# Query and key transposes from rearranged squares, relative decays, and a different start, in a fused retention and feed-forward kernel

## The chip, the core and the metric

The kernel runs on one core of one Trainium2 chip. The metric is the time of one execution on the device in microseconds (us), as the median of several runs. A profile of one execution shows the core's engines: PE is the matrix engine (PEld are its weight loads), DVE the vector engine, ACT the scalar engine, POOL the general engine, and SP the one that issues nearly all DMAs, on one queue (q1). A name with q behind it, such as SPq, is an engine's sequencer at work on instructions that are not counted as busy time, such as DMA issues.

## The reference

```python
batch, n_heads, seq, head_dim = (8, 8, 576, 64)          # q, k, v
scores = (1.0 / np.sqrt(D_)) * np.matmul(q, k.transpose(0, 1, 3, 2))
gamma = 1.0 - 2.0 ** (-5.0 - np.arange(H, dtype=np.float32))
rel = pos[:, None] - pos[None, :]
Dmat = np.where(rel >= 0, gamma[:, None, None] ** rel[None, :, :], 0.0)
attn = np.matmul(scores * Dmat[None], v)                  # (B, H, S, D)

x = attn.transpose(0, 2, 1, 3).reshape(4608, 512)
h = x @ w_in                                              # w_in 512 x 2048, float64
sp = np.maximum(h, 0.0) + np.log1p(np.exp(-np.abs(h)))
out = (h * erf(sp)) @ w_out                               # w_out 2048 x 512, float64
```

A retention layer (causal attention with one decay factor per head and no softmax) is followed by a feed-forward block. The inputs q, k, v are float32; the two weight matrices arrive as 64-bit floats and the kernel makes 32-bit floats of them itself ("rounding" below).

## The kernel before, in words

**Pieces and stages.** The retention is worked through in 40 pieces: 8 batches of 576 tokens, each cut into pieces of 128, 128, 128, 128 and 64 tokens. A piece has three stages. `transposes(i)` brings q and k into the layout with the head dimension on the partitions. `scores(i)` multiplies them and masks the product with the triangle `tri`. `outputs(i)` adds two terms in PSUM: masked scores times values (L323), and the running state times q (L334). It also multiplies keys with values (`kv`, L346) to bring the state up to date, and writes the result, scaled, into the token tile `x`. The stages are laid one over the other: transposes of piece i+1 come ahead of outputs of piece i, and scores of piece i+1 behind them. `attend(n)` issues stages up to number n, and `done[0]` counts them.

**Decays.** A power of gamma is split over two factors. Values are multiplied on POOL by a power that falls with the token's position in the whole batch (`weigh_values`, L276, table `gk`, which has one set for each of the five pieces). Outputs are multiplied by `gs` (start of the piece) and `gq` (position in it), in four instructions for a piece (L376). The state is a plain sum: for the first piece of a batch ACT copies `kv` into it (L358), later DVE adds `kv` to the old one (L360, L364).

**Transposes.** k is always transposed on PE, four matmuls with an identity for a piece (L296, tile `pt_k`), and ACT copies the result out of PSUM (L297). q goes the same way in batches 0 and 1. From batch 2 on, `load_squares` (L120, called at the first piece of the batch before) fetches the q of a whole batch by four DMAs in runs of 128 bytes (L125), laid out in squares of 32 by 32, so that one DVE instruction (L299), which transposes each 32 by 32 square, leaves the piece's q in the wanted layout.

**Loads.** `load(i)` issues the DMAs of a piece on SP (L115). Pieces 0 to 2 are asked for ahead of everything; at `transposes(i)` piece i+3 is asked for. The tiles of raw k and v have four buffers, raw q has two, so q is asked for one piece later than k and v.

**Weights.** `load_weights` fetches one part of a weight matrix (0.5 MB, L200) into one of three raw buffers. The generator `rounding` turns it into float32 in five steps a part: two ACT instructions (L217, L218), three steps of DVE (L222, L226, L230), then a last one with DVE (L235), two POOL instructions (L236, L237) and the load of a further part. After the last part of a group of four come four DVE additions (`sums_in` or `sums_out`), one a step. Four parts make the `wa` of a group (for `w_in`), four the `wb` (for `w_out`). `round_weights(n)` issues n such steps into the instruction streams at that point.

**Feed-forward.** The 4608 tokens are 9 chunks of 512, and the inner width is 4 groups; `order` takes all chunks for group 0, then for group 1 and so on. Each pair is a `First` (7 products of a Strassen-like scheme on `wa`, L432, and the activation with Softplus and Erf) and a `Second` (7 products on `wb`, L511). The retention runs among the feed-forward of group 0, a chunk ahead of it: `run` issues one or two stages ahead of each product. Results of a group are added up through `od` in DRAM.

**The start.** Up to the end of the first 512 tokens only retention stages are issued, one at a time, with two rounding steps after each from the second stage on (L585 to L587). Then come the products of `firsts[0]`, with two stages before each and one rounding step, then 4, 2 and 4 more steps around `firsts[1].first()`, and 9 at n == 1 (L620).

All engines take their instructions in the order in which the program issues them; nothing reorders them later. PSUM holds four tiles for the retention (`ps_at`), two for `a` and one each for `e` and `g`.

Of the kernel before, what the change touches and what calls it, by code (L numbers as in the profile page):

```python
# [11 lines left out]
FP32 = mybir.dt.float32  # L12
# [3 lines left out]
ALU = mybir.AluOpType  # L16
PSUM = bass.MemoryType.PSUM

P = 128
B, H, S, D = 8, 8, 576, 64  # L20
D_MODEL, D_FF = 512, 2048
NP = H // 2
NS = -(-S // P)
CONST_COLS = NS * H + NP * P + NS * NP + P

# [6 lines left out]
def decays():  # L32


    gamma = 1.0 - 2.0 ** (-5.0 - np.arange(H, dtype=np.float64))
    pairs = gamma.reshape(2, NP)
    t = np.arange(P)
    starts = np.arange(NS) * P
    gk = pairs.T.reshape(1, 1, H) ** -(starts[None, :, None] + t[:, None, None])
    row = pairs.repeat(D, axis=0)  # L40
    gq = row[:, :, None] ** t[None, None, :] / math.sqrt(D)
    gs = row[:, None, :] ** starts[None, :, None]
    tri = t[None, :] >= t[:, None]
    return np.concatenate([x.reshape(P, -1) for x in (gk, gq, gs, tri)], axis=1).astype(np.float32)
# [3 lines left out]
def kernel(  # L48
# [28 lines left out]
    wraw = ctx.enter_context(tc.tile_pool(name="wraw", bufs=3))  # L77
# [21 lines left out]
    loaded = {i: {} for i in range(len(pieces))}  # L99
# [3 lines left out]
    SQ = 32  # L103

    def load(i, names="kv"):
        if i >= len(pieces):
            return
        b, s0, n = pieces[i]
        for name, src in (("q", q), ("k", k), ("v", v)):
            if name in names and not (name == "q" and b >= SQUARES):  # L110
                bufs = 2 if name == "q" else 4
                t = raw.tile([P, H, D], FP32, tag=name, name=f"raw_{name}", bufs=bufs)
                for e in range(2):
                    heads = src[b, e * NP : (e + 1) * NP, s0 : s0 + n, :]
                    nc.sync.dma_start(out=t[:n, e::2, :], in_=heads.rearrange("h p d -> p h d"))  # L115
                loaded[i][name] = t

    squares = {}

    def load_squares(b):  # L120
        if SQUARES <= b < B:
            t = squares[b] = raw.tile([P, NP, S // SQ, SQ], FP32, tag="q4", name="raw_q4", bufs=2)
            for part in range(P // SQ):
                e, d0 = part // 2, part % 2 * SQ
                nc.sync.dma_start(  # L125
                    out=t[part * SQ : (part + 1) * SQ].rearrange("r p a d -> r (p a) d"),
                    in_=q[b, e * NP : (e + 1) * NP, :, d0 : d0 + SQ].rearrange("p (a r) d -> r (p a) d", r=SQ),
                )

    load(0, "qkv")  # L130
# [3 lines left out]
    for m in (NS * H, NP * P, NS * NP, P):  # L134
        ends.append(ends[-1] + m)
    gk, gq, gs, tri = (cst[:, a:b] for a, b in zip(ends, ends[1:]))
    gk = gk.rearrange("p (s h) -> p s h", s=NS)
    gq = gq.rearrange("p (a i) -> p a i", a=NP)
    load(1, "qkv")
# [103 lines left out]
    for _ in range(3):  # L243
        load_weights()
# [18 lines left out]
    x = {}  # L263
# [7 lines left out]
    def weigh_values(i):  # L271

        if i < len(pieces):
            _, s0, n = pieces[i]
            t = loaded[i]["v"]
            nc.gpsimd.tensor_tensor(  # L276
                out=t[:n],
                in0=t[:n],
                in1=gk[:n, s0 // P, :].unsqueeze(2).to_broadcast([n, H, D]),
                op=ALU.mult,  # L280
            )

    def transposes(i):
        b, s0, n = pieces[i]
        t = live[i] = loaded.pop(i)
        load(i + 3)
        load(i + 2, "q")
        if s0 == 0:
            load_squares(b + 1)
        weigh_values(i + 1)  # L290
        for name in "qk":
            tT = t[name + "T"] = att.tile([P, NP, P], FP32, tag=name + "T", name=name + "T")
            if name in t:
                pt = ps_at.tile([P, NP, P], FP32, tag="at", name=f"pt_{name}")
                for p in range(NP):
                    nc.tensor.transpose(pt[:, p, :n], flat(t[name][:n, 2 * p : 2 * p + 2, :]), ident[:n, :n])  # L296
                nc.scalar.copy(out=tT[:, :, :n], in_=pt[:, :, :n])  # L297
            else:
                nc.vector.transpose(  # L299
                    out=tT[:, :, :n].rearrange("p a (s i) -> p a s i", i=SQ),  # L300
                    in_=squares[b][:, :, s0 // SQ : (s0 + n) // SQ, :],
                )
# [14 lines left out]
    def outputs(i):  # L317
# [24 lines left out]
        if s0 + n < S:  # L342
            kv = ps_at.tile([P, NP, D], FP32, tag="at", name="kv")
            for p in range(NP):
                for e in range(2):
                    nc.tensor.matmul(  # L346
                        kv[e * D : (e + 1) * D, p, :],
                        lhsT=t["k"][:n, 2 * p + e, :],
                        rhs=t["v"][:n, 2 * p + e, :],
                        start=(p == 0),  # L350
                        stop=(p == NP - 1),
                        skip_group_check=True,
                    )
            old = kept.get("state")
            if pieces[i + 1][2] > D:
                new = att.tile([P, NP, D], FP32, tag="state", name="state")
                if s0 == 0:
                    nc.scalar.copy(out=new, in_=kv)  # L358
                else:
                    tt(new, kv, old, ALU.add)  # L360
            else:
                new = states[b % 2]
                for r in heads:
                    tt(new[r, :, r], kv[r], old[r], ALU.add)  # L364
            kept["state"] = new
        t0 = b * S + s0
        while t0 < b * S + s0 + n:
# [6 lines left out]
            for p in range(NP):  # L374
                j = s0 // P * NP + p
                nc.vector.scalar_tensor_tensor(  # L376
                    out=x[0, c][:, p, at],
                    in0=o[:, p, a : a + m],
                    scalar=gs[:, j : j + 1],
                    in1=gq[:, p, a : a + m],  # L380
                    op0=ALU.mult,
                    op1=ALU.mult,
                )
# [198 lines left out]

    weigh_values(0)
    while done[0] < stages_for(TCH):
        attend(done[0] + 1)  # L585
        if done[0] >= 2:
            round_weights(2)  # L587
# [5 lines left out]
    def run(steps, rounds=(), stages=1):  # L593

        for step, _ in enumerate(steps):
            attend(min(done[0] + stages, most[0]))
            if step in rounds:
                round_weights()

    run(firsts[0].first(), (0, 1), 2)  # L600
    run(firsts[0].middle(), (0, 1, 2), 2)
    run(firsts[0].last(), (0, 1), 2)
# [4 lines left out]
    round_weights(4)  # L607
    run(firsts[1].first(), (0, 1))
    firsts[0].multiply()
    round_weights(4)  # L610
    for b, nxt in zip(blocks[1:], blocks[2:] + [None]):
        n = order.index((b.g, b.c))
        if isinstance(b, First):
# [4 lines left out]
            run(b.middle(), (0, 1))  # L618
            firsts[n - 1].sums()
            if n == 1:  # L620
                round_weights(9)
            run(seconds[n - 1].first(), (0, 1))
            run(b.last())
            most[0] = stages_for(min((n + 3) * TCH, n_tok)) - (n + 3 < n_ch)
        elif n + 2 < n_s:
# [8 lines left out]
            run(nxt.first(), (0,))  # L634
            f.multiply()
            run(b.last(), (1,))
# [41 lines left out]
```

## Time and profile before

| quantity | value |
|---|---|
| median of 9 runs | 1090.33 us (1088.39 to 1091.72) |
| time of the profiled execution | 1088.99 us |
| its span | 1087.2 us |
| busy: PE, PEld, DVE, ACT, POOL | 1049.9, 901.1, 625.8, 397.0, 123.5 us |
| moved by DMA | 178.6 MB, 164 GB/s over the span |
| PE busy between 0 and 27 us | 11.71 us |
| PE busy between 27 and 54 us | 19.88 us |
| PE busy between 82 and 109 us | 21.98 us |
| PE busy between 136 and 1000 us | all of it |

The profile lists, for each group of instructions, its line, engine and operation, the tile it writes and those it reads, its shape and count, the busy time, the mean of one, and the idle time of the engine ahead of it with what ended that. In the timeline each row has the start, the time it took, engine, line, operation, tiles, count, and in brackets the idle time before it with the releaser. A row of windows has the stretch, its length, busy time and number of instructions of PE, PEld, DVE, ACT and POOL, the granted clock of PE as a share of full speed, the mean busy share of the 16 DMA engines (over 1 where packets of an engine overlap) and GB/s. With a tile named, the engines' columns count that tile's instructions alone.

### The profile page before, as it was taken

To read this page: it belongs to the slowest core of one execution; us is meant where nothing else is said; L and a number is where in the kernel's file an instruction comes from. 1 tells how busy PE (TensorE), PEld (TensorE's weight loads), DVE (VectorE), ACT (ScalarE), POOL (GpSimd) and SP (SyncE) were. 2 spreads that over 40 slices of the span, in tenths; PEclk is the share of its full clock that TensorE was granted. 3 is DMA by queue.
4 is the path that set the end of the run, shared out by engine and by line. 5 is a ranking of instruction groups with operands and counts; after the bars stand their busy time and mean duration, and the time that the engine had idled before them with its cause. 6 is when DMAs were issued, how large, how long until landed. Compare 5 with 4: busy or idle time off the path is not lost.

```text
span 1087.2 us, 15783 instructions
## 1 busy us (share of the span) xinstructions
PE 1049.9 (97%) x6472; PEld 901.1 (83%) x6472; DVE 625.8 (58%) x1074; ACT 397.0 (37%) x501; POOL 123.5 (11%) x110
## 2 busy tenths in 40 slices
PE   4798999999999999999999999999999999999996
PEld 3586788888888888888888888888888888888885
DVE  3748677587577664555555555555555545445444
ACT  2224323414414244433334444333344433333340
POOL 3314221221121000001001000010010000000000
PEclk8989899999999999999999999999999999999999
DMA  9687585574743253355555533555543333444432
GB/s 201 165 203 177 114 218 159 119 201 124 166 161 101 86 194 107 145 184 203 201 208 191 184 146 145 184 201 202 201 180 145 145 146 145 178 182 191 175 116 78
DMA packets 170377, 178.60 MB, mean 164 GB/s; under 512 B 144449, under 2 KB 144449, under 8 KB 162241
## 3 DMA queue, kind: packets, MB, share of 16 engines
q1 hardware_dynamic: 170160, 177.23, 51.5%
q8 instruction: 51, 0.84, 0.3%
q10 hardware_dynamic: 144, 0.36, 0.1%
q14 instruction: 22, 0.17, 0.1%
HBM read 123.30 MB, written 54.26 MB: 163 GB/s over the span
## 4 chain that ended last, share of the span: by engine, by line
PE 93%; DVE 3%; DMA 1%; SPq 1%; issue 1%; POOL 0%; ACT 0%; DVEq 0%; POOLq 0%; ACTq 0%
PE a L511 23%; PE a L432 23%; PE g L511 12%; PE g L432 11%; PE e L511 6%; PE e L432 5%; PE s L311 3%; PE o L323 3%; PE o L334 3%; PE kv L346 2%; PE pt_k L296 1%; SPq L115 1%; DMA raw_q<-in_q_dram 1%; DVE t L92 1%; DMA wraw<-in_moe_w_in_dram 0%
## 5 line engine op out<-in xcount | busy, mean ns | idle before, releaser
L432 PE MATMUL a<-x,wa 128*128 128x256 f32 x1152 | 275.7, 382 | 0.0
L432 PEld LDWEIGHTS a<-x,wa 128*128 128x128 f32 x1152 | 217.2, 191 | 30.5 <-issue 0.4
L511 PE MATMUL a<-wb,s 128*128 128x256 f32 x864 | 205.9, 381 | 2.3 <-DVE o L92 2.3
L511 PEld LDWEIGHTS a<-wb,s 128*128 128x128 f32 x864 | 162.5, 190 | 26.1 <-DVE o L92 2.4
L92 DVE TENSOR_TENSOR t<-g,t 128x512 f32<-128x512 f32 x72 | 49.8, 691 | 161.6 <-ACT t L462 117.6
L432 PE MATMUL g<-x,wa 128*128 128x256 f32 x576 | 137.2, 381 | 0.0
L92 DVE TENSOR_TENSOR o<-a,o 128x512 f32<-128x512 f32 x108 | 74.3, 688 | 106.4 <-PE a L511 105.6
L432 PEld LDWEIGHTS g<-x,wa 128*128 128x128 f32 x576 | 108.2, 190 | 14.8
L236 POOL TENSOR_TENSOR wraw<-wraw 128x512 f32<-128x512 f32 x32 | 34.0, 1063 | 549.2 <-DVE wraw L235 313.8
L457 ACT COPY t<-a 128x512 f32<-128x512 f32 x36 | 21.1, 586 | 195.3 <-PE a L432 195.3
L92 DVE TENSOR_TENSOR t<-t,s 128x1024 f32<-128x1024 f32 x72 | 85.8, 1233 | 0.0
L474 ACT ACTIVATE s<-t 128x1024 f32<-128x1024 f32 x72 | 72.1, 1048 | 28.3 <-DVE t L92 28.3
L511 PE MATMUL e<-wb,t 128*128 128x256 f32 x288 | 69.7, 385 | 4.9 <-POOL wb L237 4.9
L468 ACT COPY t<-a 128x512 f32<-128x512 f32 x36 | 21.1, 586 | 143.2 <-PE a L432 143.2
L479 ACT ACTIVATE s<-s 128x1024 f32<-128x1024 f32 x72 | 72.1, 1049 | 0.4
L511 PE MATMUL a<-wb,t 128*128 128x256 f32 x288 | 68.6, 381 | 1.9 <-DVE t L92 1.9
L432 PE MATMUL e<-x,wa 128*128 128x256 f32 x288 | 68.6, 381 | 0.0
L511 PE MATMUL g<-wb,t 128*128 128x256 f32 x288 | 68.6, 381 | 0.0
L511 PE MATMUL g<-wb,s 128*128 128x256 f32 x288 | 68.5, 380 | 0.0
L276 POOL TENSOR_TENSOR raw_v<-raw_v,cst 128x512 f32<-128x512 f32 (+1 forms) x40 | 47.9, 1203 | 156.0 <-DMA raw_v<-in_v_dram 116.7
L511 PEld LDWEIGHTS e<-wb,t 128*128 128x128 f32 x288 | 54.6, 192 | 12.8 <-POOL wb L237 5.3
L511 PEld LDWEIGHTS a<-wb,t 128*128 128x128 f32 x288 | 54.1, 190 | 9.7 <-DVE t L92 2.3
(59 smaller groups left out, 1201.3 us busy)
## 6 DMA issues: line engine op xcount, KB each, us to landing
x<-xd SPq DMA_DIRECT2D x27, 1792.0 KB, 11.0
od<-o SPq DMA_DIRECT2D x54, 512.0 KB, 3.9
o<-od SPq DMA_DIRECT2D x27, 1024.0 KB, 7.2
xd<-x SPq DMA_DIRECT2D x9, 1792.0 KB, 6.4
out_dram<-o SPq DMA_DIRECT2D x18, 512.0 KB, 2.8
raw_k<-in_k_dram SPq DMA_DIRECT2D x64, 128.0 KB, 3.7
raw_v<-in_v_dram SPq DMA_DIRECT2D x64, 128.0 KB, 3.3
wraw<-in_moe_w_in_dram SPq DMA_DIRECT2D x32, 256.0 KB, 4.6
```

Source lines behind the costliest of these rows:

```text
L92: nc.vector.tensor_tensor(out=out, in0=in0, in1=in1, op=op)
L236: nc.gpsimd.tensor_tensor(out=r_f, in0=high_f, in1=r_f, op=ALU.mult)
L276: nc.gpsimd.tensor_tensor(out=t[:n], in0=t[:n], in1=gk[:n, s0 // P, :].unsqueeze(2).to_broadcast([n, H, D]), op=ALU.mult,)
L311: nc.tensor.matmul(ps[e][:n, p, :n], lhsT=t["kT"][r, p, :n], rhs=t["qT"][r, p, :n], start=True, stop=True)
L323: nc.tensor.matmul(o[e * D : (e + 1) * D, p, :n], lhsT=t["v"][:n, 2 * p + e, :], rhs=t["sT"][:n, e, p, :n], start=(p == 0), stop=(s0 == 0 ...
L334: nc.tensor.matmul(o[r, p, :n], lhsT=kept["state"][r, p, :], rhs=t["qT"][r, p, :n], start=False, stop=(p == NP - 1), skip_group_check=True,)
L346: nc.tensor.matmul(kv[e * D : (e + 1) * D, p, :], lhsT=t["k"][:n, 2 * p + e, :], rhs=t["v"][:n, 2 * p + e, :], start=(p == 0), stop=(p == ...
L432: nc.tensor.matmul(acc[:, j * TH : (j + 1) * TH], lhsT=weights["wa", self.g][:, a, d, j * P : (j + 1) * P], rhs=x[self.g, self.c][a][:, d, :],
L457: nc.scalar.copy(out=self.t1[:, 1], in_=self.a)
L474: nc.scalar.activation(self.s[:, j], t, AF.Softplus)
L479: nc.scalar.activation(self.s[:, j], self.s[:, j], AF.Erf)
L511: nc.tensor.matmul(acc[:, tp, :], lhsT=left[:, j * TH + tp * P : j * TH + (tp + 1) * P], rhs=weights["wb", self.g][:, b, j, :], start=(sta ...
```

## The change

From batch 2 on, both q and k are transposed by DVE. At the second piece of a batch (`s0 == P`) `make_squares` copies the q and the k of the whole next batch from DRAM to DRAM, four DMAs each, in runs of 128 bytes, into a tile that lies in squares. `load` then fetches a piece of q and of k from there (`raw_q4`, `raw_k4`), and k also in its plain layout, which `kv` needs. All raw tiles have four buffers, so q is asked for together with k and v, three pieces ahead.

The decays are relative to the start of a piece. Values get one set of factors, outputs are multiplied by `gq` alone (one instruction for a piece, or two where it lies in two chunks), and the state is multiplied by `gp`, gamma to the power 128, at every step: DVE adds `kv` and the old state into `sums`, POOL multiplies into the new state. For the first piece of a batch DVE multiplies `kv` straight from PSUM; the ACT copy is gone.

Raw weights have four buffers, and all four parts of the first `wa` are asked for at the start. Rounding steps begin at the sixth stage, three after each, and all steps of the first `wb` are issued among the products of `firsts[0]` and right behind them; the 9 steps at n == 1 are gone. PE gets nine matmuls of the identity with itself, into a PSUM tile that nobody reads, ahead of the first stage, and two after each of the first five stages.

```diff
-CONST_COLS = NS * H + NP * P + NS * NP + P
+CONST_COLS = H + NP * P + NP + P
...
-    wraw = ctx.enter_context(tc.tile_pool(name="wraw", bufs=3))
+    wraw = ctx.enter_context(tc.tile_pool(name="wraw", bufs=4))
...
+    def make_squares(b):
+        if SQUARES <= b < B:
+            for name, src in (("q", q), ("k", k)):
+                t = squares[b, name] = dram.tile([P, NP, S // SQ, SQ], FP32, tag="sq" + name, name="sq" + name, bufs=B)
+                for part in range(P // SQ):
+                    e, d0 = part // 2, part % 2 * SQ
+                    nc.sync.dma_start(
+                        out=t[part * SQ : (part + 1) * SQ].rearrange("r p a d -> r (p a) d"),
+                        in_=src[b, e * NP : (e + 1) * NP, :, d0 : d0 + SQ].rearrange("p (a r) d -> r (p a) d", r=SQ),
+                    )
+
+    def load(i):
...
+        for name in "qk":
+            if b >= SQUARES:
+                t[name + "4"] = raw.tile([P, NP, P], FP32, tag="q" if name == "q" else "k4", name=f"raw_{name}4", bufs=4)
+                a = slice(s0 // SQ, (s0 + n) // SQ)
+                nc.sync.dma_start(
+                    out=t[name + "4"][:, :, :n].rearrange("p a (s d) -> p a s d", d=SQ), in_=squares[b, name][:, :, a, :]
+                )
         for name, src in (("q", q), ("k", k), ("v", v)):
-            if name in names and not (name == "q" and b >= SQUARES):
-                bufs = 2 if name == "q" else 4
-                t = raw.tile([P, H, D], FP32, tag=name, name=f"raw_{name}", bufs=bufs)
+            if name + "4" not in t or name == "k":
+                t[name] = raw.tile([P, H, D], FP32, tag=name, name=f"raw_{name}", bufs=4)
...
-    for _ in range(3):
+    for _ in range(4):
         load_weights()
...
     def transposes(i):
...
         load(i + 3)
-        load(i + 2, "q")
-        if s0 == 0:
-            load_squares(b + 1)
+        if s0 == P:
+            make_squares(b + 1)
         weigh_values(i + 1)
         for name in "qk":
             tT = t[name + "T"] = att.tile([P, NP, P], FP32, tag=name + "T", name=name + "T")
-            if name in t:
+            if name + "4" in t:
+                nc.vector.transpose(out=tT[:, :, :n], in_=t[name + "4"][:, :, :n])
+            else:
                 pt = ps_at.tile([P, NP, P], FP32, tag="at", name=f"pt_{name}")
...
-            old = kept.get("state")
-            if pieces[i + 1][2] > D:
-                new = att.tile([P, NP, D], FP32, tag="state", name="state")
-                if s0 == 0:
-                    nc.scalar.copy(out=new, in_=kv)
-                else:
-                    tt(new, kv, old, ALU.add)
-            else:
+            half = pieces[i + 1][2] == D
+            sums = kv
+            if s0 > 0:
+                sums = att.tile([P, NP, D], FP32, tag="sums", name="sums")
+                tt(sums, kv, kept["state"], ALU.add)
+            if half:
                 new = states[b % 2]
                 for r in heads:
-                    tt(new[r, :, r], kv[r], old[r], ALU.add)
+                    nc.gpsimd.tensor_tensor(out=new[r, :, r], in0=sums[r], in1=gp[r], op=ALU.mult)
+            else:
+                new = att.tile([P, NP, D], FP32, tag="state", name="state")
+                (nc.gpsimd if s0 > 0 else nc.vector).tensor_tensor(out=new, in0=sums, in1=gp, op=ALU.mult)
             kept["state"] = new
...
-            for p in range(NP):
-                j = s0 // P * NP + p
-                nc.vector.scalar_tensor_tensor(
...
-                )
+            tt(x[0, c][:, :NP, at], o[:, :, a : a + m], gq[:, :, a : a + m], ALU.mult)
...
+    idle = ps_e.tile([P, W], FP32, tag="g", name="idle")
+
+    def keep_busy(n):
+        for j in range(n):
+            nc.tensor.matmul(idle[:, :P], lhsT=ident, rhs=ident, start=True, stop=True)
+
+    keep_busy(9)
     weigh_values(0)
     while done[0] < stages_for(TCH):
         attend(done[0] + 1)
-        if done[0] >= 2:
-            round_weights(2)
+        if done[0] <= 5:
+            keep_busy(2)
+        if done[0] >= 6:
+            round_weights(3)
     operands_x(0, 0)
...
-            if step in rounds:
-                round_weights()
+            round_weights(rounds[step] if step < len(rounds) else 0)
...
-    run(firsts[0].first(), (0, 1), 2)
-    run(firsts[0].middle(), (0, 1, 2), 2)
-    run(firsts[0].last(), (0, 1), 2)
+    run(firsts[0].first(), (3, 3), 2)
+    run(firsts[0].middle(), (3, 3, 3), 2)
+    run(firsts[0].last(), (3, 3), 2)
...
-    round_weights(4)
-    run(firsts[1].first(), (0, 1))
+    round_weights(3)
+    run(firsts[1].first(), (1, 1))
     firsts[0].multiply()
-    round_weights(4)
...
-            if n == 1:
-                round_weights(9)
-            run(seconds[n - 1].first(), (0, 1))
+            run(seconds[n - 1].first(), (1, 1))
```

## The prediction

> **What bounds the kernel now.** I read the page's slices first, then windows of the first 140 us, the timeline where PE stood idle there, and the groups of the lines that the change touches.
>
> ```profile
> PE   4798999999999999999999999999999999999996
> PEclk8989899999999999999999999999999999999999
> DMA  9687585574743253355555533555543333444432
> ...
> PE 93%; DVE 3%; DMA 1%; SPq 1%; issue 1%; POOL 0%; ACT 0%; DVEq 0%; POOLq 0%; ACTq 0%
> ```
>
> PE is full from the fourth slice on and makes 93% of the chain that ended last, so from there a microsecond of PE work is one of the span. In the first four slices it stands, has less than its full clock in places, and DMA is at its busiest.
>
> ```profile
> 16.48 0.66 ACT L217 ACTIVATE wa<-wraw 128x512 f32<-128x512 f32 x1 [8.15 <-DMA wraw<-in_moe_w_in_dram]
> 18.07 0.59 ACT L297 COPY kT<-pt_k 128x512 f32<-128x512 f32 x1
> 18.71 1.56 PE L311 MATMUL s<-qT,kT 64*128 64x128 f32 x16 [4.78 <-ACT kT L297]
> 24.56 1.09 PE L296 MATMUL pt_q<-ident,raw_q 128*128 128x128 f32 x4 [4.29 <-DMA raw_q<-in_q_dram]
> ...
> 107.20 1.35 POOL L236 TENSOR_TENSOR wraw<-wraw 128x512 f32<-128x512 f32 x1 [3.30 <-DVE wraw L235]
> 109.94 1.90 DVE L92 TENSOR_TENSOR wb<-wb 128x512 f32<-128x512 f32 x3 [2.29 <-POOL wb L237]
> 109.96 2.07 PE L511 MATMUL e<-wb,t 128*128 128x256 f32 x4 [4.90 <-POOL wb L237]
> ```
>
> The timeline shows three stalls. The copy of kT stands on ACT behind a rounding step that waits for weights (L217): PE idles 4.78 us. The q of piece 2, asked for late, costs 4.29 us. At 105 the first products on `wb` wait for the last rounding steps.
>
> ```profile
> L296 PE MATMUL pt_k<-ident,raw_k 128*128 128x128 f32 (+1 forms) x160 | 24.3, 277 | 0.8 <-DVE x L376 0.7
> L299 DVE STREAM_TRANSPOSE qT<-raw_q 128x512 f32<-128x512 f32 (+1 forms) x30 | 19.4, 646 | 0.0
> L376 DVE SCALAR_TENSOR_TENSOR x<-o,cst 128x128 f32<-128x128 f32 (+1 forms) x176 | 44.7, 318 | 18.4 <-PE o L334 12.3 <-PE o L323 5.8
> L276 POOL TENSOR_TENSOR raw_v<-raw_v,cst 128x512 f32<-128x512 f32 (+1 forms) x40 | 47.9, 1203 | 156.0 <-DMA raw_v<-in_v_dram 116.7
> ...
> 62.13 5.07 SPq L125 DMA_DIRECT2D raw_q<-in_q_dram  x4
> 99.47 7.83 SPq L125 DMA_DIRECT2D raw_q<-in_q_dram  x4
> ...
> 235.82 0.60 PE L296 MATMUL pt_k<-ident,raw_k 128*128 128x128 f32 x4
> 236.26 1.89 PE L432 MATMUL a<-x,wa 128*128 128x256 f32 x8
> ```
>
> The groups give prices per instruction, the SP rows what four squares take to issue, and the last pair what a piece's k transposes hold PE: the next product starts 0.44 us on.
>
> **The change part by part,** in the profiled execution's own time: 1088.99 us, of which 1087.2 are span. The median of the runs shown is 1.3 above it.
>
> *k transposes.* Pieces 10 to 39 lose theirs: 24 of 128 tokens at 0.44 us, and 6 of 64 tokens at 0.39 (226.48 to 226.87 in the timeline). That is 10.6 + 2.3 = **12.9 us less** PE path, almost all behind 114 us where PE waits for nothing. DVE gets 30 more transposes, 19.4 us, as L299 shows for q. It is relieved of 176 instructions of L376 (44.7 us) for 48 multiplications out of PSUM; at the 0.63 us of the masking of scores (629 ns mean, same shape) these are 25 to 30 us, so DVE stays within 5 us of its 625.8 and at some 0.7 of the steady part. ACT loses 30 copies of 0.54 us. Neither is at its limit; nothing is counted for them.
>
> *Start, up to the first product at 42.64.* With rounding from the sixth stage on, ACT's copies no longer stand behind weights, and q of piece 2 is asked for among the first 18 DMAs. Both stalls, 9.1 us, can go. What is late next is piece 3: ahead of it and with it on the one queue lie three pieces (2.3 MB), the constants (0.3), four weight parts instead of three (2.1) and itself (0.8), 5.5 MB. The windows of 3 to 21 us show 214 to 260 GB/s, so it lands at about 27 us. POOL then has the weighing of piece 3, and behind it in the same queue a state multiplication and the rounding of four parts (1.04 + 1.29 us each): 27 + 1 + 0.6 + 2.3 + 1 + 2.3 = 34 for part 1, and the second state behind that. The first product moves to about 38: **4 us less**, between 0 (POOL's queue takes it all) and 9.1. The nine identity matmuls run while PE waits for its first data until 5.42, and the ten others, some 0.2 us each by the rate of a 128 x 256 product (1.73 us for eight instructions, two to a product), where PE stood: nothing to 2 us, inside these ends.
>
> *Products of the first chunk, 43 to 86.* DVE gets 24 rounding steps of `wb` here, 17 more than before, at 0.42 to 0.69 us: about 9 us into a stretch in which it was 12.14 busy of 28 (54 to 82). PE's short stop at 51 and the half clock after it (0.50 between 54 and 60) came from a DVE queue that is much the same in the new order. Counted at 0; ends 4 less (the clock stays up) and 3 more.
>
> *The stall at 105.* PE stands from 105 to 110 for `wb`, takes four instructions more slowly until 114, where the clock is back; by the product's usual 1.73 us and a full clock that stretch is worth 9 us. In the new order all `wb` steps come ahead of the second chunk's `first()`, so this wait goes: **9 us less**. But its successor is in view. POOL's queue now reads: weighing of piece 10, then the last two instructions of `wb`, and DVE's three remaining `wb` sums behind these. Piece 10 is the first of batch 2: its v is asked for on SP behind `raw_q4`, which waits for the new squares. Those are asked for at piece 6, behind piece 9's loads, at about 66.8 - 4 = 62. At the row's price eight squares take 10 to 16 us to issue, and landing (median 4.7 from issue) ends 3 later: 75 to 81. Six DMAs at 0.5 and a landing of 3.3 bring v at 82 to 87, POOL needs 3.4: 85 to 90. DVE stands there at about 91 - 4 = 87. So 0 to 3 us come back if a DMA from DRAM to DRAM goes at the rate of the one into SBUF; at double the price per square 13 to 19. No row shows such a copy. I take **3 us back**, since run length, bytes and queue are those of L125.
>
> The Trainium skill, DMA: Bandwidth & Descriptors, Specifications, speaks against this: it wants at least 512 bytes for line rate and names a read-modify-write below that. The trace's squares also moved in runs of 128 bytes, into SBUF, in 5 to 8 us for 1.2 MB; no run here shows runs of 128 bytes written to DRAM. If the rule doubled the square's price, the sum below would be that of the second rival, not of the forecast.
>
> *DMA in the steady part.* Between 114 and 380 the mean DMA share is 0.55; a batch lasts 44 to 46 us (L125 at 149.2, 193.6, 240.2, 286.0), so 24 us of it. Added are four more squares (7 us) and 2.4 MB of `raw_q4` and `raw_k4` at some 300 GB/s (8 us): 39 of 44, a share of 0.88, where stretches of 1.2 are on record. From piece 1 of a batch to piece 0 of the next PE takes 36 us; squares, the loads ahead of them and the four tensors behind take 23 to 30. Hidden, by 6 us. POOL's state multiplication, new on the path from `kv` to the next outputs, has about 0.5 us (half of the 1.04 of L276) and stands behind a weighing that may wait for v; some of that will show: **1 us more**, ends 0 and 40 (eight late for each of five batches, at double the price).
>
> Sum: -12.9 - 4 + 0 - 9 + 3 + 1 = -22, so 1088.99 - 22 = 1067, and 1068 as a median.
>
> **The rivals.**
> 1. *The stall only changes its cause.* The start gains nothing, and v of piece 10 comes 9 us late: only the transposes count, 1090.3 - 13 + 1 = 1078. For it: POOL's queue in the new order, DMA shares near or above 1.0 from 54 to 70. Against it: 5 to 10 us between the old and the new places of the steps.
> 2. *Slower: copies from DRAM to DRAM at double the price.* At piece 10, 16 us come instead of 3, then 33 to 44 us are needed where 36 are there: 0 to 8 late in each of five batches, say 4, 20 together. -12.9 - 4 - 9 + 16 + 20 + 1 = +11, so 1101. Over the forecast that is 33 dearer (13 and 20), so it decides from about 1.7 times the row's price, where two thirds of the 33 use up the 22. For it: steady DMA use would pass 1.0. Against it: the queue's rate with large stores, 401 GB/s in the window 225 to 228, shows no dearer write.
> 3. *Everything hides.* The start gains 9, the clock 4, nothing comes back: -12.9 - 9 - 4 - 9 = -35, 1055.
>
> **How the numbers follow.** Forecast (1060 to 1075) 0.50, rival 1 (1075 to 1088) 0.18, rival 3 (below 1060) 0.14, rival 2 and whatever else is slower 0.14, in between 0.04. The runs shown spread by 0.3%, so 0.2% is about what can be told from no change. Faster 0.82, same 0.04, slower 0.14. From 1053 to 1089 there lies some 0.82; the forecast's own range is 1060 to 1075.
>
> **What would show it.** No `pt_k` behind 90 us and the same products closer together: right for the transposes. PE without a wait for `wb` near 105; a wait for a weighing, for `raw_v` or `raw_k4` in its place is rival 1. Four squares that take over 10 us to issue, DMA shares above 1 in the steady part and DVE waiting for `raw_k4` at every first piece of a batch are rival 2. The prediction is wrong if PE is no longer full behind 130 us.

## The result and the profile after

| | before | after |
|---|---|---|
| median, us | 1089.66 (33 runs) | 1095.92 (11 runs, 1092.02 to 1098.46) |
| ratio to before | | 1.0053 [1.0043, 1.0062] |
| profiled execution and its span, us | 1088.99, 1087.2 | 1097.34, 1095.6 |
| busy: PE, DVE, ACT, POOL, us | 1049.9, 625.8, 397.0, 123.5 | 1048.8, 622.0, 379.4, 141.9 |
| moved by DMA | 178.6 MB | 199.8 MB |
| packets | 170,377 | 257,734 |

The changed kernel is slower by 0.5%. It was forecast to be 2% faster (1068), and its time lies outside the range of 1053 to 1089.

First the slices of the span and the chain that ended last, of the kernel after:

```profile
PE   7796999999997999999999999999999999999996
PEclk9897999899998999999999999999999999999999
DMA  9889999999999444344455543545554333455432
...
PE 81%; SPq 8%; DMA 5%; DVE 2%; POOL 2%; issue 1%; ACT 0%; POOLq 0%; DVEq 0%; ACTq 0%
```

A slice is 27.4 us. Before, the DMA digits lay between 2 and 8 from the fifth slice to the fourteenth; now they read 9 up to the thirteenth. PE is no longer nearly the whole chain: SP's issuing and DMA hold 13% of it, and the fourth slice (82 to 109 us) has a 6 and a lowered clock.

Two windows say what became of the steady part. The columns are those explained for before: busy time and count of PE, PEld, DVE, ACT and POOL, granted clock, DMA share, GB/s. Of the kernel after:

```profile
82.00:109.00 27.00, 18.34 (x141) 14.98 (x140) 15.41 (x26) 6.46 (x10) 8.92 (x7) 0.75 1.00 226
136.00:350.00 214.00, 200.78 (x1759) 164.30 (x1758) 140.08 (x240) 53.30 (x67) 45.97 (x50) 0.95 0.97 227
```

The same stretch of the kernel before:

```profile
136.00:350.00 214.00, 214.00 (x1940) 175.54 (x1942) 150.73 (x307) 69.76 (x99) 38.10 (x34) 1.00 0.59 153
```

Behind 136 us PE had no idle time before and now has 13.2 us, and the clock falls to 0.95 on the mean. The DMA share rises from 0.59 to 0.97, where 0.88 was predicted.

The timeline of PE after shows where it stands (idle time and releaser in brackets):

```profile
26.18 1.08 PE L299 MATMUL pt_q<-ident,raw_q 128*128 128x128 f32 x4 [6.21 <-DMA raw_q<-in_q_dram]
...
37.62 2.46 PE L321 MATMUL o<-sT,raw_v 128*64 128x128 f32 x16 [3.42 <-issue]
...
99.39 1.44 PE L321 MATMUL o<-sT,raw_v 64*64 64x64 f32 x16 [8.66 <-DVE sT L90]
...
193.48 1.97 PE L332 MATMUL o<-qT,state 128*128 128x64 f32 x8 [3.97 <-POOL state L360]
...
341.34 1.97 PE L332 MATMUL o<-qT,state 128*128 128x64 f32 x8 [6.08 <-POOL state L360]
```

Of the three old stalls, the one for `kT` and the one for `wb` are gone from PE. The one for a late q has moved from piece 2 to piece 3 and grown to 6.21 us. A stop of 3.42 us for the mask of piece 3 follows at 37.62, and the first product starts at 42.44 (42.64 before). Two kinds are new: 8.66 us at 90.7 to 99.4, and four stops, 12.0 us together, at products that read the state.

**The stop at 91 us.** Followed back, it begins on SP. The queue's rows of the kernel after:

```profile
64.48 1.26 SPq L132 DMA_DIRECT2D raw_q<-in_q_dram  x2
65.84 1.26 SPq L132 DMA_DIRECT2D raw_k<-in_k_dram  x2
67.14 1.27 SPq L132 DMA_DIRECT2D raw_v<-in_v_dram  x2
68.46 6.02 SPq L110 DMA_DIRECT2D sqq<-in_q_dram  x4
74.53 8.08 SPq L110 DMA_DIRECT2D sqk<-in_k_dram  x4
82.78 1.42 SPq L124 DMA_DIRECT2D raw_q<-sqq  x1
86.06 0.57 SPq L124 DMA_DIRECT2D raw_k<-sqk  x1
86.67 1.75 SPq L132 DMA_DIRECT2D raw_k<-in_k_dram  x2
88.46 1.06 SPq L132 DMA_DIRECT2D raw_v<-in_v_dram  x2
```

Piece 9's own six loads take 4.0 us ahead of the copies. Eight copies take 14.1 us to issue. `raw_q4` is queued behind them, `raw_k4` starts 1.9 us after that one has been issued, and v of piece 10 is queued behind both. POOL and DVE, same kernel:

```profile
92.87 1.04 POOL L281 TENSOR_TENSOR raw_v<-raw_v,cst 128x512 f32<-128x512 f32 x1 [13.95 <-DMA raw_v<-in_v_dram]
93.87 1.04 POOL L240 TENSOR_TENSOR wraw<-wraw 128x512 f32<-128x512 f32 x1
94.99 1.27 POOL L241 TENSOR_TENSOR wb<-wb,wraw 128x512 f32<-128x512 f32 x1
96.30 2.70 DVE L90 TENSOR_TENSOR wb<-wb 128x512 f32<-128x512 f32 x3 [8.02 <-POOL wb L241]
98.92 0.74 DVE L90 TENSOR_TENSOR sT<-s,cst 64x256 f32<-64x256 f32 x2
```

POOL stands 13.95 us for that v; the rounding of `wb` is queued behind its weighing; DVE stands 8.02 us for `wb`, and the masking of scores that PE needs next is queued behind DVE's three sums. PE names `sT` as its releaser, and `sT` is only the last of five links.

**The stops behind 136 us.** The first of them, on SP and POOL of the kernel after:

```profile
166.10 6.50 SPq L110 DMA_DIRECT2D sqq<-in_q_dram  x4
172.64 7.29 SPq L110 DMA_DIRECT2D sqk<-in_k_dram  x4
180.10 1.84 SPq L124 DMA_DIRECT2D raw_q<-sqq  x1
184.84 0.57 SPq L124 DMA_DIRECT2D raw_k<-sqk  x1
...
186.66 1.06 SPq L132 DMA_DIRECT2D raw_v<-in_v_dram  x2
...
191.13 1.04 POOL L281 TENSOR_TENSOR raw_v<-raw_v,cst 128x512 f32<-128x512 f32 x1 [16.51 <-DMA raw_v<-in_v_dram]
192.13 1.29 POOL L360 TENSOR_TENSOR state<-sums,cst 64x256 f32<-64x256 f32 x2
```

Here the weighing of the next batch's first v (L281) stands ahead of the state that the last piece of this batch needs (L360). From the first copy to the weighed v it is 26 us (166.10 to 192.17). At 193.48 PE goes on.

How much earlier the state is due than the next batch's first outputs shows at a batch boundary of the same kernel without a stop:

```profile
147.34 1.10 PE L332 MATMUL o<-qT,state 128*128 128x64 f32 x8
...
154.90 1.09 PE L321 MATMUL o<-sT,raw_v 128*64 128x128 f32 x16
```

That is 7.6 us.

The groups that answer to those of before, in the kernel after:

```profile
L295 DVE STREAM_TRANSPOSE kT<-raw_k 128x512 f32<-128x512 f32 (+1 forms) x30 | 18.5, 616 | 0.9 <-DMA raw_k<-sqk 0.9
L90 DVE TENSOR_TENSOR x<-o,cst 128x512 f32<-128x512 f32 (+1 forms) x44 | 25.4, 585 | 20.2 <-PE o L332 20.2
```

The k transposes on DVE took 18.5 us (19.4 predicted) and the output scaling 25.4 (25 to 30 predicted); these prices were right. `pt_k` is left for 10 pieces of 40.

### The profile page after: what moved, and what is told of

It reads as the page before. It is cut to its first block, busy times and chain, and to the rows that moved or that the text cites. A ratio compares the mean times of both kernels' runs of the same rounds, so it can differ in the third digit from the quotient of the medians.

```text
span 1095.6 us, 15530 instructions
## 1 busy us (share of the span) xinstructions
PE 1048.8 (96%) x6390; PEld 902.0 (82%) x6390; DVE 622.0 (57%) x972; ACT 379.4 (35%) x463; POOL 141.9 (13%) x142
## 2 busy tenths in 40 slices
DMA packets 257734, 199.79 MB, mean 182 GB/s; under 512 B 207232, under 2 KB 231808, under 8 KB 249600
## 4 chain that ended last, share of the span: by engine, by line
PE 81%; SPq 8%; DMA 5%; DVE 2%; POOL 2%; issue 1%; ACT 0%; POOLq 0%; DVEq 0%; ACTq 0%
PE a L501 21%; PE a L422 21%; PE g L422 11%; PE g L501 11%; PE e L501 5%; PE e L422 5%; SPq L132 3%; SPq L110 3%; PE s L309 2%; PE o L321 2%; PE o L332 2%; DMA raw_v<-in_v_dram 2%; DMA sqk<-in_k_dram 2%; DMA wraw<-in_moe_w_in_dram 1%; PE kv L344 1%
## 5 line engine op out<-in xcount | busy, mean ns | idle before, releaser
L422 PE MATMUL g<-x,wa 128*128 128x256 f32 x576 | 140.1, 387 | 0.0
L422 PEld LDWEIGHTS g<-x,wa 128*128 128x128 f32 x576 | 110.5, 194 | 15.7
L447 ACT COPY t<-a 128x512 f32<-128x512 f32 x36 | 21.1, 586 | 203.2 <-PE a L422 203.2
L458 ACT COPY t<-a 128x512 f32<-128x512 f32 x36 | 21.1, 586 | 159.5 <-PE a L422 159.5
L281 POOL TENSOR_TENSOR raw_v<-raw_v,cst 128x512 f32<-128x512 f32 (+1 forms) x40 | 45.6, 1140 | 191.5 <-DMA raw_v<-in_v_dram 187.6
L452 ACT COPY t<-a 128x512 f32<-128x512 f32 x36 | 21.1, 585 | 128.6 <-PE a L422 128.6
```

Source lines behind the costliest of these rows:

```text
L281: nc.gpsimd.tensor_tensor(out=t[:n], in0=t[:n], in1=gk[:n, :].unsqueeze(2).to_broadcast([n, H, D]), op=ALU.mult)
L422: nc.tensor.matmul(acc[:, j * TH : (j + 1) * TH], lhsT=weights["wa", self.g][:, a, d, j * P : (j + 1) * P], rhs=x[self.g, self.c][a][:, d, :],
```

## The experiments

In all of them the kernel before ran beside the others, at 1089.0 to 1089.4 us, so the medians of the different sets can be set side by side. Differences are from the kernel after unless another is named.

**1. No copies at all.** Theory: the copies cause both new kinds of stall, and all else in the change is a gain. Rival: something else in the change (rounding, decays, POOL's state) costs by itself.

```diff
-    SQUARES = 2
+    SQUARES = B
```

> The changed kernel with q and k transposed on PE in all eight batches: no squares, no raw_q4 and raw_k4. Against the kernel before, PE gets the q transposes of pieces 10 to 39, 13 us. Theory S (the squares' DMAs cost what the start and the shorter PE path gain): PE no longer waits for a weighing or a state between 85 and 350, the wait for wb near 105 stays away, and the start shows its gain of up to 9: 1090 + 13 - 9 = 1094, or 1094 to 1099, with the first products of the second chunk in step with the kernel before or earlier. Theory T (the new start or the relative decays cost by themselves): 1105 or more, with waits of PE that the kernel before does not have.

Measured: 1093.34, ratio to before 1.0035 [1.0023, 1.0048]. Between 85 and 1000 us PE has 0.5 us of idle time. In this kernel q and k of all 40 pieces are transposed on PE; before it was k alone in the last 30, so by the row of before (0.44 and 0.39 us a piece) PE carries 12.9 us more. What is left of the change is worth 1089.0 + 12.9 - 1093.3 = 8.6 us. So start, decays and rounding together are a gain, and the loss belongs to the copies: they take 25.8 us of work off PE and still end 2.6 us later, so the stalls that they bring cost some 28 by these prices. That is an estimate; experiment 3 measures 26.

**2. The state on DVE.** Theory: in the steady part the copies hurt only because the state is queued behind a weighing on POOL. Rival: DMA is simply too full, and another wait steps in.

```diff
-                    nc.gpsimd.tensor_tensor(out=new[r, :, r], in0=sums[r], in1=gp[r], op=ALU.mult)
+                    tt(new[r, :, r], sums[r], gp[r], ALU.mult)
...
-                (nc.gpsimd if s0 > 0 else nc.vector).tensor_tensor(out=new, in0=sums, in1=gp, op=ALU.mult)
+                tt(new, sums, gp, ALU.mult)
```

> The changed kernel with the state's multiplication by gp on DVE instead of POOL. Theory P (POOL's queue hands its wait for v on to the state): PE's waits for the state behind POOL, 12 us in four, go, and DVE's 32 multiplications of 0.4 us lie beside PE: 1084 to 1089. Theory Q (what is late is the data of the piece itself, and the state only comes first in line): the same four places wait for sT, kT or the weighed v instead, 1094 to 1098. The wait of DVE for wb behind the weighing of piece 10 (8 us) stays in both.

Measured: 1083.53, 0.9948 [0.9936, 0.996], which is 12.4 us less. On DVE and PE of this kernel:

```profile
95.64 1.90 DVE L90 TENSOR_TENSOR wb<-wb 128x512 f32<-128x512 f32 x3 [6.28 <-POOL wb L241]
...
97.97 1.40 PE L321 MATMUL o<-sT,raw_v 64*64 64x64 f32 x16 [7.08 <-issue]
...
238.34 2.08 PE L309 MATMUL s<-qT,kT 64*128 64x128 f32 x16 [4.29 <-DVE kT L295]
```

The waits for the state are gone, with the copies and the DMA load as they were (share 1.00 between 136 and 350 us). One stop of 4.29 us, for a k from the squares, shows that the next limit is near. The stop at 91 us stays, with 7.08 us: it goes through `wb`, not through the state.

**3. The same bytes in long runs.** The eight copies move the same 2.4 MB, but in long runs. The tile then doesn't hold squares, so the transposes of q and k are in effect left out.

```diff
-                        out=t[part * SQ : (part + 1) * SQ].rearrange("r p a d -> r (p a) d"),
-                        in_=src[b, e * NP : (e + 1) * NP, :, d0 : d0 + SQ].rearrange("p (a r) d -> r (p a) d", r=SQ),
+                        out=t[part * SQ : (part + 1) * SQ].rearrange("r p a d -> r (p a d)"),
+                        in_=src[b, part * 2 : part * 2 + 2].rearrange("p s d -> (p s d)").rearrange("(r x) -> r x", r=SQ),
```

> The changed kernel, but the copies from DRAM to DRAM move the same bytes in long contiguous runs, so that the tiles do not hold squares (the transposes of q and k are left out in effect; all instructions stay). Theory R (runs of 128 bytes make the copies dear): issue of a copy falls from 1.6 to 1.8 us to under 1, the DMA share between 82 and 350 falls from 0.9 to 1.06 to about 0.75, the stalls at the batch boundaries go: 1070 to 1080. Theory L (the place in SP's queue, with its waits for landing, costs, whatever the rate): within 4 us of the changed kernel.

Measured: 1070.35, 0.9822 [0.9807, 0.9837]. SP's rows of this kernel, for the first batch of copies, and its steady window:

```profile
66.48 2.50 SPq L109 DMA_DIRECT2D sqq<-in_q_dram  x4
69.03 2.48 SPq L109 DMA_DIRECT2D sqk<-in_k_dram  x4
```

```profile
136.00:350.00 214.00, 214.00 (x1949) 175.84 (x1949) 156.31 (x263) 59.09 (x75) 52.61 (x53) 1.00 0.82 232
```

Eight copies issue in 5 us instead of 14, and PE has no idle time between 95 and 1000 us, with POOL's order untouched. The time is 25.6 us below the kernel after. So the loss comes from how long the copies take, not from their place in SP's queue. The time to issue them and the time until they land fell together, and no run separates the two. That the time is within 2.4 us of the forecast is in part luck: neither the 4 us that the start was to gain nor the 4 us that the sum had for the copies came. The Trainium skill, DMA: Bandwidth & Descriptors, Specifications, which asks for at least 512 bytes for line rate, agrees in direction: here the runs of 128 bytes took nearly three times as long to issue as the same bytes in long ones.

**4. The squares asked for two pieces ahead.** Theory: it is the order on SP that hurts, v standing behind `raw_q4` and `raw_k4`. Here these two are asked for one piece later, behind the plain k and v of the piece after. Rival: the squares themselves come too late.

```diff
         load(i + 3)
+        load_squares(i + 2)
```

`load` keeps the plain tiles, and `load_squares` issues the two loads that were at its head.

> The changed kernel with raw_q4 and raw_k4 asked for two pieces ahead instead of three, behind the k and v of the piece three ahead, which therefore no longer stand on SP behind the wait for the squares. Theory L (SP's order keeps v back): POOL's weighing of a batch's first piece and all behind it come 5 us earlier, most of PE's 21 us of waits behind 85 us go: 1076 to 1086. Theory B (the DMA engines are full, in any order): DVE waits for raw_q4 or raw_k4 in place of POOL's wait for v, 1092 to 1100.

Measured: 1098.59, 1.0084 [1.0069, 1.0099]: slower than the kernel after. The list of PE's waits and two rows of the timeline of this kernel:

```profile
PE s L316 <- DVE kT L302: 17.2, 5, 5.6
```

```profile
133.88 2.08 PE L316 MATMUL s<-qT,kT 64*128 64x128 f32 x16 [5.64 <-DVE kT L302]
182.64 1.53 PE L316 MATMUL s<-qT,kT 64*128 64x128 f32 x16 [4.20 <-DVE kT L302]
```

The stop at 91 us shrinks to 3.50 us and no product waits for the state, but the wait moves to the first scores of each of five batches: DVE stands for `raw_q4`, which the edit itself asks for a piece later (36.2 us in seven waits), and transposes k only behind it. So this order on SP, with the copies as long as they are, only changes who waits.

**5. Which part costs how much.** Two kernels leave batch 2 on PE, so that the copies begin one batch later, when the start is over; with the state on POOL and on DVE they make a square of four with the kernel after and experiment 2.

```diff
-    SQUARES = 2
+    SQUARES = 3
```

> The changed kernel with one number different: squares from batch 3 on (state's multiplication on POOL as in the change). The stall near 91 goes, 8.7 us and the half clock behind it, less 4.5 us for q and k of five pieces on PE, as state on DVE has shown (13 us less); the four waits for the state behind POOL stay, less one at most (9 to 12 us). Theory P (both causes add up): 1096 - 13 = 1083. If the two are one and the same wait: 1070 to 1075.

> State's multiplication on DVE and squares from batch 3 on, asked for as in the changed kernel. Only the first batch of copies falls away, and with it the stall near 91 (7 us and some half clock); q and k of five pieces go back to PE, 4.5 us. Theory L and theory B alike: 1078 to 1082; if the stall near 91 has another cause it stays and the time is 1086 to 1089.

| median, us | copies from batch 2 | copies from batch 3 |
|---|---|---|
| state on POOL | 1095.92 | 1080.67, 0.992 [0.9907, 0.9934] |
| state on DVE | 1083.53 | 1070.43, 0.9825 [0.9805, 0.9846] |

Leaving out the first batch of copies saves 15.2 and 13.1 us, although it gives PE 4.3 us of transposes back (8 times 0.44 and 2 times 0.39). Moving the state saves 12.4 and 10.2. Together they save 25.5, and neither depends on the other by more than the noise of these few runs. Both new kernels came out lower than expected, the one with the state on DVE by 8 us or more. The expectations had priced the stop at 91 us alone, but the later stops shrink too: with the state on POOL from four to two (12.0 to 4.4 us), with it on DVE the one of 4.29 us goes. So the 13 to 15 us are not all the stop at 91. In the kernel of the lower right corner PE has 0.9 us of idle time between 95 and 1000 us, with a DMA share of 1.00 between 136 and 350.

**6. Copies spread out and a batch earlier.** State on DVE, copies from batch 3, two of them at each of four pieces, asked for a batch earlier.

```diff
-        if s0 == P:
-            make_squares(b + 1)
+        if s0 < 4 * P:
+            make_squares(b + 2, s0 // P)
```

> State's multiplication on DVE, batch 2 transposed on PE like 0 and 1, and from batch 3 on the squares asked for a batch earlier, two copies at each of the first four pieces. Theory L (each copy is paid for only where something stands on SP's wait for all eight): no wait for landing on SP, no stall at batch boundaries and at 90: 1083.5 - 7 (stall at 91) - 6 (stall at 234 with its half clock) + 4.5 (q and k of five pieces on PE) = 1075, 1070 to 1079. Theory B (DMA engines are full, the order does not matter): stalls come back at other places, 1082 to 1090.

Measured: 1069.92, 0.9824 [0.9807, 0.9841], not to be told from the 1070.43 without the spreading. Once the state is off POOL, the steady copies are hidden and nothing more is to be had there.

**7. Only q from squares, k on PE** (state on DVE).

```diff
-            for name, src in (("q", q), ("k", k)):
+            for name, src in (("q", q),):
...
-        for name in "qk":
+        for name in "q":
```

> State's multiplication on DVE, and squares of q alone: four copies and one raw_q4 a piece; k transposed on PE as in the kernel before. PE gets the 12.9 us back. Theory L and B: with half the copies the stalls at 91 and 234 shrink to 0 to 4 of some 14: 1083.5 + 12.9 - 10 to 14 = 1083 to 1087. If the transposes of k on PE cost less than the spacing of products says, it is under 1080.

Measured: 1082.86, 0.9943 [0.9931, 0.9956]. No stop over 1.4 us is left behind 85 us, and the time lies 12.5 above the one of experiment 3, where PE has no stop behind 95 us either. In the traces, from the `kv` of piece 8 to the last one, it takes 279.1 us here (84.65 to 363.74) and 267.0 there (83.56 to 350.51), 12.1 more. The two kernels also differ in the state's engine and in the runs of q's copies, but neither stands for them. That is close to the 12.9 of the prediction's first term. Beside experiment 2 (1083.53), k's squares gain nothing that can be told: what they take off PE, the longer copies cost again.

**8. No matmuls of the identity** (state on DVE).

```diff
-        for j in range(n):
+        for j in range(0):
```

> State's multiplication on DVE, and no matmuls of the identity (19 left out; their result is read by nobody). Theory N (they lie where PE would wait and what comes next waits for data): within 1.5 us of the kernel with them, 1082 to 1085. Theory W (they keep the clock up and so shorten the first stages, and what follows): 2 to 5 us slower, with the granted clock lower up to 27 us.

Measured: 1084.22, 0.9956 [0.9944, 0.9969], against 0.9948 [0.9936, 0.996] with them. No effect that can be told. Up to 20 us the granted clock was 1.00 in both kernels.

**9. The old numbers of rounding steps** (state on DVE, copies from batch 3).

```diff
-        if done[0] >= 6:
-            round_weights(3)
+        if done[0] >= 2:
+            round_weights(2)
...
-    run(firsts[0].first(), (3, 3), 2)
+    run(firsts[0].first(), (1, 1), 2)
```

and likewise for the other numbers of before, the 9 steps at n == 1 among them.

> Squares from batch 3 on and the state's multiplication on DVE, with the numbers of rounding steps at each place as in the kernel before (four raw weight buffers and the early loads of q stay). Theory E (the stall at 105 of the kernel before was the late wb steps alone): it comes back, PE waits 5 to 7 us for wb near 105 and runs at half clock behind it, ACT's copy of kT stands behind the weights again: 1070.4 + 6 to 9 = 1076 to 1080. Theory D (shorter DVE work through the relative decays had already made room): 1069 to 1073.

Measured: 1075.59, 0.9865 [0.9846, 0.9885], 5.2 above the 1070.43 without this edit. PE's timeline of this kernel has two of the old stalls back:

```profile
20.99 2.08 PE L309 MATMUL s<-qT,kT 64*128 64x128 f32 x16 [7.83 <-ACT kT L300]
...
107.73 2.07 PE L501 MATMUL e<-wb,t 128*128 128x256 f32 x4 [4.27 <-POOL wb L241]
```

But the first product comes at 43.24, against 43.42 without the edit: at the start the new numbers gain nothing. The traces divide the rest. At the `kv` of piece 10 the kernel with the old numbers is 3.1 us ahead (101.77 against 104.85), at that of piece 11 it is 4.3 us behind (119.32 against 115.00). So the stall at 105 us, with its clock of 0.50 up to 112, costs 7.4 us where the prediction had 9, and the new numbers give back 3.1 of that on the way there. Only the rounding steps were moved here; the early loads of q, the four raw buffers and the matmuls of the identity were in both kernels.

**10. Piece 3 ahead of two weight parts** (state on DVE, copies from batch 3).

```diff
-    for _ in range(4):
+    for _ in range(2):
         load_weights()
...
+        if done[0] == 1:
+            for _ in range(2):
+                load_weights()
```

> Squares from batch 3 on and the state's multiplication on DVE, with the loads of weight parts 3 and 4 moved behind those of piece 3. PE's wait for the q of piece 3 (7 us near 20 to 27) becomes some 4 us shorter, as 1 MB less lies ahead of it. Theory M (the start is paced by that q): the first product comes 3 us earlier, 1066 to 1069. Theory O (POOL's rounding of the later parts is next in line): the first or second product stays where it was, 1069 to 1073.

Measured: 1067.75, 0.9807 [0.9787, 0.9827]: the fastest kernel of the study, 2% faster than before. Its timeline at the start:

```profile
22.57 0.63 PE L299 MATMUL pt_q<-ident,raw_q 128*128 128x128 f32 x4 [2.77 <-DMA raw_q<-in_q_dram]
...
35.95 1.99 PE L422 MATMUL a<-x,wa 128*128 128x256 f32 x8
```

The wait for q of piece 3 falls from 7.06 to 2.77 us and the first product comes at 35.95 instead of 43.42. A second wait, 5.8 us for the state's sums at 44.4, stands behind it, yet at the `kv` of piece 8 this trace is 5.2 us ahead (80.49 against 85.65) and at the end 6.8. But the two traces are of one of the fastest runs of this kernel (1066.15) and the slowest of the other (1073.05). The medians differ by 2.7 us, with intervals that overlap. That the weight parts delayed piece 3 is shown; what it is worth, 3 or 7 us, is not.

## Why the prediction was wrong

**k transposes, -12.9: right.** 12.5 by the medians of experiment 7, 12.1 by its trace.

**Start, -4: wrong, little of it came.** The step foresaw the successor (piece 3, behind four weight parts) and put its landing at 27 us, which was right (26.18). The mistake was in what follows. The step followed POOL's queue alone, and had the first product at 38; the trace has 42.44. POOL had the state that piece 3 needs at 37.39, where the step's list has it soon after 34. But PE stood 3.42 us until 37.62 already ahead of that state's product, for the masking of piece 3's scores on DVE. Three rounding steps stood ahead of it there, from 33.60 to 36.84, and two of them took 1.4 us each, against 0.68 and 0.43 for the same steps at 20.76 and 21.48. Behind these stops the granted clock was 0.50 from 27 to 31 us and 0.57 from 38 to 42. Neither the mask behind the rounding nor the clock was in the step. Experiment 10 shows the weight parts as the cause of the late q. By the products of the first chunk the kernel after is 1.4 us ahead (84.47 against 85.89), so start and first chunk together were worth 1.4 in place of 4.

**Stall at 105, -9: the mechanism right, the size somewhat too large.** The stall for `wb` goes where the copies don't interfere. It was worth 7.4 us in the traces of experiment 9, and 5.2 by the medians with what the new numbers cost ahead of it. All parts but the copies together gave 8.6 in experiment 1, where the sum had 13.

**Three us back at piece 10: the chain right, the time and the price of lateness wrong.** v behind `raw_q4` on SP, POOL's weighing ahead of the last rounding of `wb`, DVE's sums behind that: it came out link by link as the step had it. The price of a copy was also right, 14.1 us for eight within the predicted 10 to 16. But the step took its start from "66.8 - 4 = 62", and the copies began at 68.46. Of these 6.5 us, 4.0 are piece 9's six loads, which the step named as ahead of the copies and gave no time; the other 2.5 come from the start, which had gained little of its 4. They went straight through: POOL was done with the weighing and `wb` at 96.3, not at 85 to 90. The half clock behind such a stop, which the step on the old stall had counted, was not counted for the new one. Experiment 5 has 13 to 15 us for this first batch of copies and the later stops that shrink with it, after the 4.3 us of PE work that its loss would bring, instead of 3. This is rival 1 in its mechanism.

**Steady DMA, "Hidden, by 6 us": the step that failed.** The need was priced right, 26 us in the trace for "23 to 30". The deadline was wrong. The step took 36 us, from piece 1 to piece 0 of the next batch, as if the first piece of the next batch were the first to wait. But in POOL's queue the weighing of that first piece stands ahead of the state for the *last piece of the current batch*, which PE reads 7.6 us before the next batch's first outputs (147.34 and 154.90). So some 28 us were there, and the boundary without a stop has just that (119.01 to 147.34). In the four batches with a stop the copies also began later against PE: it ran out of work 23.4 to 27.1 us behind the first copy, and the state came after 27.4 to 30.5. The next sentence of the prediction names this very place, the state that "stands behind a weighing that may wait for v", and prices it at 1 us, with an upper end of 40. Experiment 2 measures 12.4 and experiment 5 10.2. The two sentences were never put together: with 28 in place of 36, the step's own 23 to 30 is no longer hidden by 6 us. The four stops were 0.4 to 6.1, and a lowered clock followed them.

**DVE, ACT, decays, identity matmuls at nothing.** For the matmuls this is right within the noise (experiment 8). DVE's and ACT's busy times came out as forecast, and behind 136 us neither cost anything in experiment 3, where PE never stood; at the start DVE did cost something, as said above. No run takes the decays by themselves.

**Rival 2** had the sign and a time 5 us off, and its cause was wrong: the copies didn't cost double the row's price. Slower came from two places at the normal price, which the list of cases had only as "whatever else is slower". With cheap copies (experiment 3), or with the two places mended (experiment 5), the kernel takes 1070, where the sum said 1068.

## What to carry to other kernels

When an instruction is put on an engine that waits for transfers, look for the first instruction *behind* that wait whose result is needed, and count the deadline from there; the one that waits is often not the first one due. Start times that an earlier term of the sum has moved are as uncertain as that term: carry its worst end through every later deadline. A stage with stops in it is better judged by taking the transfer's length away, as in experiment 3, than by the releaser that PE names.

## What the runs showed of the hardware

**Half the clock behind stops of 1.5 and 1.9 us.** Windows of the kernel after around the stop of 1.53 us that ended at 241.43:

```profile
239.00:240.00 1.00, 0.91 (x18) 0.54 (x16) 0.00 (x0) 0.58 (x1) 0.91 (x1) 1.00 1.02 295
240.00:241.00 1.00, 0.00 (x0) 0.00 (x0) 0.00 (x0) 0.00 (x0) 0.93 (x3) 1.00 1.18 271
...
243.00:244.00 1.00, 1.00 (x5) 0.80 (x4) 0.11 (x1) 0.00 (x0) 1.00 (x2) 0.53 1.07 459
...
250.00:251.00 1.00, 1.00 (x6) 0.88 (x5) 1.00 (x3) 0.00 (x0) 0.00 (x0) 1.00 1.36 273
```

The granted clock drops to 0.53 at 243, some 1.6 us after PE is at work again, and is back at 250; a second stop, of 1.26 us up to 246.68, lies in between. In experiment 3 a single stop of 1.92 us, up to 92.35, was followed by 0.50 from 95 to 97. Behind one of 1.35 us, up to 94.75 in the kernel with the state on DVE and copies from batch 3, the clock stayed at 1.00. Behind the stop of 8.66 us it was 0.50 from 99 to 103 and 0.56 from 103 to 107. So a stop can cost more than its length. The steady part shows the sum of it: from the second product on `wb` to the last `kv` it took 267.2 us after (112.56 to 379.74) and 246.5 in experiment 3 (104.01 to 350.51), 20.7 more, of which PE's idle time is 13. The other 7.5 us, over five stops, go with the lowered clock (0.96 on the mean of that stretch). The Trainium skill, TensorE: Matmul & The Clock Gate, Part 1, has the half clock begin after an idle window of about 3.4 us; here the stops ahead of the drops were 1.53 and 1.92 us.

**A full DMA need not show.** With a share of 1.00 and 228 GB/s between 136 and 350 us, PE stood 0.9 us in that stretch in the kernel with the state on DVE and copies from batch 3; with 0.97 and 227 GB/s it stood 13.2 in the kernel after. The share told nothing of the loss; the queue behind one weighing did.

**Copies from DRAM to DRAM in runs of 128 bytes** took 14 to 15 us to issue for 2.4 MB, and the load that waits for the last of them began 17.6 and 18.7 us after the first (68.46 to 86.06, 166.10 to 184.84). The windows of the kernel after from 119 to 133, 166 to 180 and 213 to 228 us have 147 to 153 GB/s in all, at a share of 0.93 to 1.04. The same bytes in long runs let SP go on after 5 us.
